# The sine written over the angle, the decays of the next pair fetched earlier, and VectorE making all rows of z in the first four steps

## The chip, the cores and the metric

The kernel runs on one core of one Trainium2 chip. The metric is the device time of one execution in microseconds (us). The core has five engines with their own instruction queues: TensorE (PE; its weight loads are listed as PEld), VectorE (DVE), ScalarE (ACT), GpSimd (POOL), and SyncE (SP), which here only issues DMA transfers. Each engine works through its queue in order, and semaphores hold an instruction until its operands are ready.

## The reference

Three stages in a row: a linear attention with complex decays over 768 tokens (4 batches, 8 heads, head size 48), a dense layer pair with a leaky unit, and a routed mixture of 8 experts, of which the first best one is taken per token.

```python
mag = sqrt(a_re * a_re + a_im * a_im)
scale = minimum(mag, 0.999) / (mag + 1e-06)
for t in range(768):
    S_re, S_im = ar * S_re - ai * S_im + k[t] (x) v[t], ar * S_im + ai * S_re
    y[t] = q[t] @ S_re
h = y @ w_in                     # 3072 x 384 @ 384 x 2048
x = (maximum(h, 0) + alpha * minimum(h, 0)) @ w_out
# mixture of experts on x: e = argmax(x @ w_gate + bias), out = p_e * (relu(x @ w1[e]) @ w2[e])
```

## The kernel before

**Steps and pairs.** The 768 tokens are cut into 6 chunks of 128, and with 4 batches there are 24 steps (k = 0 to 23). A step's attention is written with running products: with the scanned angle tau and the scanned magnitude (and its inverse) of the decays, the queries and keys are multiplied by cosine and sine of the angle and by these products. The result is z, a tile [128, 2, 3, 257]: for r = 0 (cosine) and r = 1 (sine), three sets of 128 key columns (L749) and 128 query columns (L751), and one column of the chunk's end. Steps are made in pairs (0,1), (2,3), ... (22,23); pairs (0,1) and (2,3) are handled in the opening.

**polar and polar_group.** polar() loads a pair's decays wa (real and imaginary part, 768 KB) and its queries and keys wq (768 KB). polar_group() then runs some 45 instructions on DVE, ACT and POOL over four work tiles m, x, s, e, whose names repeat from pair to pair with one buffer each: squares of wa on ACT (e, L664, and m, L665), an inverse root behind a table load (x, L670, and s, L671), products on DVE (L667, L673 to L679), the sign (L686) and arctangent (L691) in place in wa, the angle scans (L715, x <- wa) and their reduction by whole turns (L723, L725), the other scans, the cosine (L734, into e) and the sine (L735, into wa, whose real part is no longer needed). L742 keeps the last angle of a step for the next chunk (carry), and L749 and L751 write z. Tile wa has one buffer, so the next pair's wa can't be loaded until the last row of z that reads the sine is done. Pairs are written out as generators, from which one DVE instruction at a time is taken and set behind the dense layer's DVE instruction of that turn.

**After z.** SP sends z to DRAM (zd) and fetches it in another layout (qk). On PE each step's attention is pa (L782), the transposes pk (L790), copied by ACT to ks (L792), then py (L800, L802) and the state update pu (L814). Two steps fill xt, the input of one unit of the dense layer.

**The dense layer** goes through 12 units of 8 groups g. A group is ph (L843 to L846) on PE, n on ACT (L851), n on DVE (L853, two rows), gh on ACT (L856), gl on POOL (L858), and two groups later acc on PE (L878). In what follows gh_5 is the gh of the sixth group of a unit, and so on. Rows lt, mx, run, ix and the indirect load tbl (L237 to L260) are the routing of finished tokens; wraw, wf and w (L551 to L610) are the dense layer's weights, decoded during the opening; the last part of the kernel is the mixture of experts (L466 to L497). Which engine makes a row is set by side(mask), a test of a mask's bit that stands for the pair (bit 1, 2 for steps 0 and 1, 4 for pair (2,3), 8 for (4,5), 16 for the rest); with DZ = 15 a cosine row of L751 is on POOL for all pairs, and a sine row is on DVE for steps 0 to 5 and on POOL later.

Of the kernel before, what the change touches and what calls it, by code (L numbers as in the profile page):

```python
# [11 lines left out]
F32 = mybir.dt.float32  # L12
# [3 lines left out]
AF = mybir.ActivationFunctionType  # L16
ALU = mybir.AluOpType
PSUM = bass.MemoryType.PSUM

B, H, S, D = 4, 8, 768, 48  # L20
CH = 128
NC = S // CH
NSTEP = NC * B
# [52 lines left out]
DZ = 15  # L76
# [18 lines left out]
class Emit:  # L95
    def __init__(self, ctx, tc, aps):
        self.ctx, self.tc, self.nc = ctx, tc, tc.nc
        self.__dict__.update(aps)
        self.raws, self.vs, self.zs, self.zd, self.queue = {}, {}, {}, {}, None
        self.behind = None  # L100
        self.nwarm = 0
        self.paced = self.sine = None
        self.pacing = True
        self.scattered = []
        self.free = {"pa": ["pa0", "pa1"], "pq": ["pq0", "pq1"]}
# [512 lines left out]
    def polar(self, ks, split=False, apart=False):  # L618


        nc, ap_ = self.nc, self.ap_
        n, k0 = len(ks), ks[0]
        T = lambda nm, *sh, bufs=1: ap_.tile([128, *sh], F32, name=f"{nm}{k0}", tag=nm, bufs=bufs)
        W = 3 * CH
        if apart:

            wa, wq, *w = [self.wp.tile([128, 2, 2, W], F32, name=f"p{k0}_{i}", tag=f"w{NFC - 1 - i}") for i in range(4)]
            work = [w[i // 2][:, i % 2] for i in range(4)]
        else:
            wa, wq = T("wa", 2, 2, W), T("wq", 2, 2, W)  # L630
            work = None
        for lo, hi in [(i, i + 1) for i in range(n)] if split else [(0, n)]:
            self.dma(wa[:, lo:hi], self.pa_[k0 + lo:k0 + hi].rearrange("k p a t -> p k a t"))
            self.dma(wq[:, lo:hi], self.pq_[k0 + lo:k0 + hi].rearrange("k p a t -> p k a t"))
        return [ks, wa, wq, work]

    def polar_run(self, st, lo, hi, inline=False):
        ks, wa, wq, work = st
        if work is None:
            work = st[3] = [self.ap_.tile([128, 2, wa.shape[3]], F32, name=f"{nm}{ks[0]}", tag=nm, bufs=1) for nm in WORK]  # L640
        return self.polar_group(ks[lo:hi], wa[:, lo:hi], wq[:, lo:hi], [w[:, lo:hi] for w in work], inline)
# [14 lines left out]
    def polar_group(self, ks, wa, wq, work, inline):  # L656
        nc, ap_ = self.nc, self.ap_
        c = ks[0] // B
        ar, ai, q, kk = wa[:, :, 0], wa[:, :, 1], wq[:, :, 0], wq[:, :, 1]
        m2, x, s, e = work  # L660
        V, G, A = nc.vector, nc.gpsimd, nc.scalar
        bit = {0: 1, 1: 2, 2: 4, 4: 8}.get(ks[0], 16)
        side = lambda mask: G if mask & bit else V
# [45 lines left out]
        tau, pp, bb = x, m2, s  # L709
        t3 = lambda ap: ap.rearrange("p (j t) -> p j t", j=3)  # L710
# [11 lines left out]
        yield from scan(tau, "angle", ai, ALU.mult, ALU.add)  # L722
        A.activation(e, tau, AF.Identity, bias=self.magic)  # L723
        yield 1
        V.scalar_tensor_tensor(tau, e, MAGIC, tau, ALU.subtract, ALU.subtract)  # L725
        yield 1

        yield
# [1 line left out]
        yield from scan(pp, "decay", m2, ALU.max, ALU.mult)  # L730
        yield
        A.activation(e, tau, AF.Abs)
        sn, cs = ar, e
        A.activation(cs, e, AF.Sin, bias=self.hpi, scale=-2.0 * PI_LO)  # L734
        self.sine = A.activation(sn, tau, AF.Sin, scale=2.0 * PI_LO).ins  # L735
        side(GD).tensor_tensor(kk, kk, bb, ALU.mult)
# [1 line left out]
        side(~DQ).tensor_tensor(q, q, pp, ALU.mult)  # L738
        for i, k in enumerate(ks):
            yield  # L740
            if c < NC - 1:
                A.activation(self.carry[:, k % B], t3(tau[:, i])[:, :, CH - 1], AF.Identity, scale=-1.0)  # L742
            zp, zt = (self.wp, f"w{9 + k // 2}") if k in (1, 3) else (ap_, "z")
            z = zp.tile([128, 2, 3, 2 * CH + 1], F32, name=f"z{k}", tag=zt, bufs=ZB if zt == "z" else 1)
            end = t3(pp[:, i])[:, :, CH - 1]
            A.copy(self.pend[:, k, :], end)
            A.copy(z[:, :, :, CH], end.unsqueeze(1).to_broadcast([128, 2, 3]))
            for r, tr in enumerate((cs, sn)):
                self.last = V.tensor_tensor(z[:, r, :, CH + 1:], t3(kk[:, i]), t3(tr[:, i]), ALU.mult).ins  # L749
                yield 1  # L750
                side(~(DZ if r else 0)).tensor_tensor(z[:, r, :, :CH], t3(q[:, i]), t3(tr[:, i]), ALU.mult)  # L751
            self.zs[k] = z
            if inline:
                self.bounce(k)
                if not BB:
                    self.bounce_back(k)
# [329 lines left out]
def body(ctx, tc, aps):  # L1086
# [117 lines left out]
    def steps(text):  # L1204

        for part in re.findall("([^0-9 ]+)([0-9]*)", text):
            for c in part[0] * int(part[1] or 1):
                if c in "<>":
                    link[0] = c == "<"
                else:  # L1210
                    with em.behind_turn() if c in PT else nullcontext():
                        (chained if link[0] else step)(c)

    gens["p"], gens["C"] = polar(4, 5), attn_unit(2)
    steps(START)
    jobs, later = {}, {}
# [28 lines left out]
    for u in range(3, NU):  # L1245
        pg, ag = polar(2 * u, 2 * u + 1), attn_unit(u)
        p0 = max(NP * (u - 1) + PO, P0 + PS * (u - 2))
        width = PE_ if u < 6 else PW
        for i in range(PN):
            at(p0 + i * width // PN, pace if PACE & 1 else op, pg, d=later)  # L1250
        shift[u - 2] = max(0, p0 + width - NP * (u - 1))
        for i, m in enumerate(AT):
            at(NP * (u - 1) + shift[u - 2] + i, arun if PACE & 2 else run, ag, m)
# [127 lines left out]
```

## Time and profile before

| | before |
|---|---|
| runs | 992.59, 994.52, 1004.37 us; median 994.52 |
| profiled execution, device time | 996.86 us |
| its span in the trace | 995.1 us |
| mean granted clock of PE | 0.928 |
| busy: PE, PEld | 854.4 (86%), 807.5 (81%) |
| busy: DVE, ACT, POOL | 658.0 (66%), 478.3 (48%), 426.6 (43%) |
| DMA | 117.81 MB, mean 118 GB/s |
| loads of wa, of wq | 10 each, 768 KB, 10.2 and 8.6 us to landing |
| zd and qk | 24 each, 771 KB, 4.7 and 8.1 us to landing |

Busy time is the time in which an engine has an instruction running. A wait is put down to what ended it last ("PE pk <- ACT ks" is PE idle until ACT's copy ks). A row with several instructions (x4) shows its first start and the time to the last one's end. The granted clock is a share of full speed.

### The profile page before, as it was taken

The page shows a single profiled execution, that of the slowest core. Times are in us where ns is not written, and L with a number is a line of the kernel's source. Part 1 is how long each engine was busy: PE and PEld are TensorE (multiplying, and loading weights), DVE is VectorE, ACT ScalarE, POOL GpSimd, SP SyncE. Part 2 cuts the span into 40 slices and gives each one's busy share as a digit, 9 for nine tenths or more (in the row PEclk, how much of TensorE's full clock was granted, in tenths as well). Part 3 has the DMA queues.
Part 4 walks back from the last instruction along what each step waited for, and adds up shares of the span by engine and source line. Part 5 has one row for each costly group of instructions (what it writes and reads, how often), then busy time and mean ns, then how long its engine had stood idle before and what let it go on. Part 6 is the DMA issues. An engine that isn't in the chain of part 4 may idle for free. (4 is left out here: it accounts for less than half of the span.)

```text
span 995.1 us, 16140 instructions
## 1 busy us (share of the span) xinstructions
PE 854.4 (86%) x5948; PEld 807.5 (81%) x5948; DVE 658.0 (66%) x1264; ACT 478.3 (48%) x870; POOL 426.6 (43%) x339
## 2 busy tenths in 40 slices
PE   0655968897966999899899989898999999999994
PEld 0655958887965898889798989898999878889994
DVE  6986885779594959495968777784455464535561
ACT  7652556464454455363736464642234434434550
POOL 1135353436252634436463636462353264244451
PEclk9855977896997999999999999999999999999998
DMA  7816500242635251716243333423032445445560
GB/s 302 263 56 205 203 9 1 84 137 63 165 108 116 80 137 30 201 31 159 75 133 101 104 112 99 131 69 104 6 113 68 139 140 173 120 142 157 191 190 19
DMA packets 61290, 117.81 MB, mean 118 GB/s; under 512 B 10201, under 2 KB 39401, under 8 KB 61201
## 3 DMA queue, kind: packets, MB, share of 16 engines
q1 hardware_dynamic: 57232, 106.91, 36.3%
q0 software_dynamic: 3968, 9.77, 3.1%
q8 instruction: 49, 0.80, 0.4%
q14 instruction: 41, 0.33, 0.1%
HBM read 85.58 MB, written 28.91 MB: 115 GB/s over the span
## 5 line engine op out<-in xcount | busy, mean ns | idle before, releaser
L858 POOL TENSOR_TENSOR gl<-n,gh 128x512 fp32r<-128x512 f32 x96 | 143.6, 1498 | 224.1 <-ACT gh L856 111.3
L843 PE MATMUL ph<-xt,w 128*128 128x256 f32 x576 | 161.0, 306 | 17.1 <-DVE n L853 14.6
L878 PE MATMUL acc<-w,gh 128*128 128x392 f32 x768 | 165.4, 354 | 9.8 <-DVE lt L237 7.2
L844 PE MATMUL ph<-xt,w 128*128 128x256 f32 x576 | 155.1, 295 | 0.0
L878 PEld LDWEIGHTS acc<-w,gh 128*128 128x128 f32 x768 | 138.8, 197 | 11.6 <-DVE lt L237 8.4
L853 DVE SCALAR_TENSOR_TENSOR n<-n,al,ph 128x256 f32<-128x256 f32 x192 | 84.5, 474 | 87.7 <-ACT n L851 87.4
L843 PEld LDWEIGHTS ph<-xt,w 128*128 128x128 f32 x576 | 116.3, 202 | 19.9 <-DVE n L853 6.7
L844 PEld LDWEIGHTS ph<-xt,w 128*128 128x128 f32 x576 | 116.9, 203 | 0.2 <-issue 0.2
L846 PE MATMUL ph<-xt,w 128*128 128x256 f32 x576 | 106.9, 296 | 0.7 <-DVE w L559 0.7
L851 ACT ACTIVATE n<-ph 128x512 f32<-128x512 f32 x96 | 57.1, 595 | 100.3 <-PE ph L846 89.0
L856 ACT CAST gh<-n 128x512 fp32r<-128x512 f32 x96 | 59.4, 619 | 89.7 <-DVE n L853 82.9
L878 PE MATMUL acc<-w,gl 128*128 128x392 f32 x384 | 89.9, 350 | 11.9 <-POOL gl L858 11.9
L846 PEld LDWEIGHTS ph<-xt,w 128*128 128x128 f32 x576 | 88.4, 203 | 1.2 <-DVE w L559 1.0
L878 PEld LDWEIGHTS acc<-w,gl 128*128 128x128 f32 x384 | 71.4, 194 | 13.4 <-POOL gl L858 13.2
L782 PE MATMUL pa<-qk 96*128 96x128 f32 x384 | 58.2, 299 | 26.2 <-DMA qk<-zd 17.0
L782 PEld LDWEIGHTS pa<-qk 96*128 96x128 f32 x384 | 53.8, 210 | 30.3 <-DMA qk<-zd 12.3
L784 DVE TENSOR_TENSOR at<-pa,mask 128x512 f32<-128x512 f32 x48 | 32.7, 682 | 40.5 <-PE pa L782 34.4
L486 DVE SCALAR_TENSOR_TENSOR hls<-p2s,hhs 128x512 fp32r<-128x512 f32 x32 | 22.1, 689 | 38.3 <-ACT hhs L485 38.3
L260 POOL DMA_INDIRECT tbl<-tok,ix x24 | 25.5, 1064 | 50.4 <-DVE run L259 24.3
L800 PE MATMUL py<-at,v 128*64 128x128 f32 x384 | 44.5, 302 | 1.5 <-DVE at L784 1.1
L467 DVE TENSOR_TENSOR wls<-wrs,whs 128x768 fp32r<-128x768 f32 x20 | 28.2, 1409 | 25.6 <-ACT whs L466 25.6
L497 PE MATMUL a2s<-wls,hhs 128*128 128x384 f32 x128 | 43.7, 341 | 0.0
(334 smaller groups left out, 2034.2 us busy)
## 6 DMA issues: line engine op xcount, KB each, us to landing
zd<-z SPq DMA_DIRECT2D x24, 771.0 KB, 4.7
qk<-zd SPq DMA_DIRECT2D x24, 771.0 KB, 8.1
wraw<-in_w_io_dram SPq DMA_DIRECT2D x16, 768.0 KB, 12.3
wrs<-in_wcat_dram SPq DMA_DIRECT2D x32, 384.0 KB, 3.2
wrf<-in_wcat_dram SPq DMA_DIRECT2D x24, 384.0 KB, 3.6
wa<-in_pa__dram SPq DMA_DIRECT2D x10, 768.0 KB, 10.2
wq<-in_pq__dram SPq DMA_DIRECT2D x10, 768.0 KB, 8.6
v<-in_vv_dram SPq DMA_DIRECT2D x24, 200.0 KB, 2.4
```

Of the source, the lines that this page charges most:

```text
L497: nc.tensor.matmul(acc[t], x[:, 128 * t:128 * t + 128], w[:, DM:], start=(f == 0 and x is hh and w is wh), stop=(last and x is hl))
L782: nc.tensor.matmul(pa[:, i, :], kt[:, h, :], qt[:, h, :CH], start=True, stop=True)
L784: self.last = nc.vector.tensor_tensor(at, pa, self.mask.unsqueeze(1).to_broadcast([128, 4, CH]), ALU.mult).ins
L800: nc.tensor.matmul(o, v[:, h * D:h * D + 64], ats[g][:, i, :], start=True, stop=(c == 0))
L843: nc.tensor.matmul(ph[:, i, :], w1(fc, 0, c), xt[:, c, 0, :], start=(c == 0), stop=False)
L844: nc.tensor.matmul(ph[:, i, :], w1(fc, 0, c), xt[:, c, 1, :], start=False, stop=False)
L846: last = nc.tensor.matmul(ph[:, i, :], w1(fc, 1, c), xt[:, c, 0, :], start=False, stop=(c == 2)).ins
L851: nc.scalar.activation(nf, ph, AF.Relu, scale=-1.0)
L853: paced = nc.vector.scalar_tensor_tensor(nf[:, i, :], nf[:, i, :], self.al1[:, 2 * p + i:2 * p + i + 1], ph[:, i, :], ALU.mult, ALU.add).ins
L856: copy = nc.scalar.copy(gh, nf).ins
L858: rest = nc.gpsimd.tensor_tensor(gl, nf, gh.bitcast(F32), ALU.subtract).ins
L878: nc.tensor.matmul(acc[t][:, :XW], x[:, i, 128 * t:128 * t + 128], self.w[2 * p + i][:, h, DM:], start=(p == i == h == 0 and x is gh), sto ...
```

## The change

The sine is written over the angle (tile x) and no longer over wa, and the carry is kept at once when the angle is reduced, ahead of the other scans. For the pairs from (4,5) to (20,21) the load of the next pair's wa is written right behind the angle scans; polar() of that next pair then only loads wq. All rows of z of steps 0 to 3 go to DVE. Behind the third hunk's lines the code of polar_group goes on as before.

```diff
--- before.py
+++ after.py
@@ -96,6 +96,7 @@
     def __init__(self, ctx, tc, aps):
         self.ctx, self.tc, self.nc = ctx, tc, tc.nc
         self.__dict__.update(aps)
+        self.ahead, self.loaded = {}, None
         self.raws, self.vs, self.zs, self.zd, self.queue = {}, {}, {}, {}, None
         self.behind = None
         self.nwarm = 0
@@ -627,12 +628,22 @@
             wa, wq, *w = [self.wp.tile([128, 2, 2, W], F32, name=f"p{k0}_{i}", tag=f"w{NFC - 1 - i}") for i in range(4)]
             work = [w[i // 2][:, i % 2] for i in range(4)]
         else:
-            wa, wq = T("wa", 2, 2, W), T("wq", 2, 2, W)
+            wa = self.ahead.pop(k0, None) or T("wa", 2, 2, W)
+            wq = T("wq", 2, 2, W)
             work = None
+            if self.loaded == k0:
+                self.dma(wq, self.pq_[k0:k0 + n].rearrange("k p a t -> p k a t"))
+                return [ks, wa, wq, work]
         for lo, hi in [(i, i + 1) for i in range(n)] if split else [(0, n)]:
             self.dma(wa[:, lo:hi], self.pa_[k0 + lo:k0 + hi].rearrange("k p a t -> p k a t"))
             self.dma(wq[:, lo:hi], self.pq_[k0 + lo:k0 + hi].rearrange("k p a t -> p k a t"))
         return [ks, wa, wq, work]
+
+    def load_ahead(self, k):
+
+        wa = self.ahead[k] = self.ap_.tile([128, 2, 2, 3 * CH], F32, name=f"wa{k}", tag="wa", bufs=1)
+        self.dma(wa, self.pa_[k:k + 2].rearrange("k p a t -> p k a t"))
+        self.loaded = k
 
     def polar_run(self, st, lo, hi, inline=False):
         ks, wa, wq, work = st
@@ -722,7 +733,12 @@
         yield from scan(tau, "angle", ai, ALU.mult, ALU.add)
         A.activation(e, tau, AF.Identity, bias=self.magic)
         yield 1
+        if 4 <= ks[0] < NSTEP - 2:
+            self.load_ahead(ks[0] + 2)
         V.scalar_tensor_tensor(tau, e, MAGIC, tau, ALU.subtract, ALU.subtract)
+        if c < NC - 1:
+            for i, k in enumerate(ks):
+                A.activation(self.carry[:, k % B], t3(tau[:, i])[:, :, CH - 1], AF.Identity, scale=-1.0)
         yield 1
 
         yield
@@ -730,7 +746,7 @@
         yield from scan(pp, "decay", m2, ALU.max, ALU.mult)
         yield
         A.activation(e, tau, AF.Abs)
-        sn, cs = ar, e
+        sn, cs = tau, e
         A.activation(cs, e, AF.Sin, bias=self.hpi, scale=-2.0 * PI_LO)
         self.sine = A.activation(sn, tau, AF.Sin, scale=2.0 * PI_LO).ins
         side(GD).tensor_tensor(kk, kk, bb, ALU.mult)
@@ -738,8 +754,6 @@
         side(~DQ).tensor_tensor(q, q, pp, ALU.mult)
         for i, k in enumerate(ks):
             yield
-            if c < NC - 1:
-                A.activation(self.carry[:, k % B], t3(tau[:, i])[:, :, CH - 1], AF.Identity, scale=-1.0)
             zp, zt = (self.wp, f"w{9 + k // 2}") if k in (1, 3) else (ap_, "z")
             z = zp.tile([128, 2, 3, 2 * CH + 1], F32, name=f"z{k}", tag=zt, bufs=ZB if zt == "z" else 1)
             end = t3(pp[:, i])[:, :, CH - 1]
@@ -748,7 +762,7 @@
             for r, tr in enumerate((cs, sn)):
                 self.last = V.tensor_tensor(z[:, r, :, CH + 1:], t3(kk[:, i]), t3(tr[:, i]), ALU.mult).ins
                 yield 1
-                side(~(DZ if r else 0)).tensor_tensor(z[:, r, :, :CH], t3(q[:, i]), t3(tr[:, i]), ALU.mult)
+                side(~(15 if ks[0] < 4 else DZ if r else 0)).tensor_tensor(z[:, r, :, :CH], t3(q[:, i]), t3(tr[:, i]), ALU.mult)
             self.zs[k] = z
             if inline:
                 self.bounce(k)
```

In the order of SP's queue, with v the values, xt a copy that completes a unit's input, and the names' first number the step, the stretch around z of pair (12,13) stands thus before and after:

```order
L651 DMA qk12_3484<-zd12_3472 96x8x257
L651 DMA zd13_3482<-z13_3475 128x1542
L651 DMA wa14_3577<-in_pa__dram 128x2x768
L651 DMA qk13_3486<-zd13_3482 96x8x257
L651 DMA wq14_3578<-in_pq__dram 128x2x768
L651 DMA v14_3581<-in_vv_dram 128x400
L651 DMA v15_3583<-in_vv_dram 128x400
```

```order
L662 DMA qk12_3486<-zd12_3475 96x8x257
L662 DMA zd13_3484<-z13_3477 128x1542
L662 DMA wq14_3579<-in_pq__dram 128x2x768
L662 DMA qk13_3488<-zd13_3484 96x8x257
L662 DMA v14_3581<-in_vv_dram 128x400
L662 DMA wa16_3816<-in_pa__dram 128x2x768
L662 DMA v15_3583<-in_vv_dram 128x400
L823 DMA xt6_3602<-t3_12_3757 16x6x128 x2
```

The load of wa for a pair stood between zd and the second qk of the pair before it; now wq stands there, and wa of the pair after stands further on, between two loads of v and ahead of the copies to xt.

In the order of ACT's queue, at the end of the groups of unit 5 (n5_, gh5_) and the start of pair (16,17) (tiles e16, m216, x16, s16), with ks14 the copy of step 14's attention:

```order
L851 ACTIVATE n5_5_4021<-ph5_5_4002 128x512
L856 CAST gh5_5_4025<-n5_5_4021 128x512
L851 ACTIVATE n5_6_4088<-ph5_6_4069 128x512
L856 CAST gh5_6_4092<-n5_6_4088 128x512
L851 ACTIVATE n5_7_4127<-ph5_7_4108 128x512
L856 CAST gh5_7_4131<-n5_7_4127 128x512
L664 ACTIVATE e16_4158<-wa16_4147 128x768
L665 ACTIVATE m216_4155<-wa16_4147 128x768
L670 ACT_TABLE_LOAD
L670 ACTIVATE x16_4156<-e16_4158,tiny_75 128x768
L671 ACTIVATE s16_4157<-m216_4155,tiny_75 128x768
L792 COPY ks14_0_4185<-pk14_0_4180 128x384
```

```order
L865 ACTIVATE n5_5_4024<-ph5_5_4005 128x512
L870 CAST gh5_5_4028<-n5_5_4024 128x512
L675 ACTIVATE e16_4158<-wa16_3816 128x768
L681 ACT_TABLE_LOAD
L681 ACTIVATE x16_4156<-e16_4158,tiny_75 128x768
L865 ACTIVATE n5_6_4090<-ph5_6_4071 128x512
L870 CAST gh5_6_4094<-n5_6_4090 128x512
L865 ACTIVATE n5_7_4129<-ph5_7_4110 128x512
L870 CAST gh5_7_4133<-n5_7_4129 128x512
L682 ACTIVATE s16_4157<-m216_4155,tiny_75 128x768
L806 COPY ks14_0_4185<-pk14_0_4180 128x384
L697 ACTIVATE wa16_3816,oks_103<-wa16_3816,mth_89 128x2x384
```

The rows e, table load and x moved from behind gh5_7 to behind gh5_5, so ahead of n5_6; m moved further up (ahead of n5_4); s stays between gh5_7 and ks14_0.

In the order of DVE's queue, at z of step 2 (z2), among the rows that decode the weights wf2 and wf3; p2_3 holds the cosine, p2_0 before and p2_2 now the sine:

```order
L749 TENSOR_TENSOR z2_450<-p2_1_125,p2_3_127 128x3x128
L749 TENSOR_TENSOR z2_450<-p2_1_125,p2_0_124 128x3x128
L601 TENSOR_SCALAR wf2_456<-wf2_456 128x768
L601 TENSOR_SCALAR wf3_457<-wf3_457 128x768
L604 TENSOR_SCALAR wf2_456<-wf2_456 128x768
L604 TENSOR_SCALAR wf3_457<-wf3_457 128x768
L607 SCALAR_TENSOR_TENSOR wf2_456<-wraw2_138,wf2_456 128x768
L607 SCALAR_TENSOR_TENSOR wf3_457<-wraw3_140,wf3_457 128x768
L610 SCALAR_TENSOR_TENSOR wf2_456<-wraw2_138,wf2_456 128x768
L610 SCALAR_TENSOR_TENSOR wf3_457<-wraw3_140,wf3_457 128x768
L751 TENSOR_TENSOR z2_450<-p2_1_125,p2_0_124 128x3x128
L749 TENSOR_TENSOR z3_472<-p2_1_125,p2_3_127 128x3x128
```

```order
L763 TENSOR_TENSOR z2_451<-p2_1_125,p2_3_127 128x3x128
L765 TENSOR_TENSOR z2_451<-p2_1_125,p2_3_127 128x3x128
L763 TENSOR_TENSOR z2_451<-p2_1_125,p2_2_126 128x3x128
L602 TENSOR_SCALAR wf2_457<-wf2_457 128x768
L602 TENSOR_SCALAR wf3_458<-wf3_458 128x768
L605 TENSOR_SCALAR wf2_457<-wf2_457 128x768
L605 TENSOR_SCALAR wf3_458<-wf3_458 128x768
L608 SCALAR_TENSOR_TENSOR wf2_457<-wraw2_138,wf2_457 128x768
L608 SCALAR_TENSOR_TENSOR wf3_458<-wraw3_140,wf3_458 128x768
L611 SCALAR_TENSOR_TENSOR wf2_457<-wraw2_138,wf2_457 128x768
L611 SCALAR_TENSOR_TENSOR wf3_458<-wraw3_140,wf3_458 128x768
L765 TENSOR_TENSOR z2_451<-p2_1_125,p2_2_126 128x3x128
```

The second row here now is step 2's cosine row of L751, which POOL made before; the same holds for step 3, whose four rows follow. POOL's queue lost these two rows and those of steps 0 and 1.

## Rows read from the trace of the kernel before

**Rows 1.** Busy time by stretch: us, busy of PE, PEld, DVE, ACT, POOL; PEclk, DMA.
```profile
200.00:333.00 133.00, 105.90 (x767) 98.12 (x767) 98.36 (x183) 66.17 (x110) 56.54 (x38) 0.87 0.40 110
345.00:676.00 331.00, 301.49 (x2398) 289.76 (x2393) 243.81 (x475) 171.75 (x295) 164.01 (x119) 0.98 0.40 110
700.00:750.00 50.00, 50.00 (x373) 49.25 (x373) 24.70 (x90) 17.14 (x30) 22.54 (x19) 1.00 0.20 59
```

**Rows 2.** PE's waits, 200 to 333 us: us in total, times, longest.
```profile
PE acc L878 <- POOL gl L858: 8.9, 3, 5.7
```

**Rows 3.** PE's waits, 345 to 680 us.
```profile
PE acc L878 <- DVE lt L237: 7.2, 6, 2.1
PE pk L790 <- ACT ks L792: 6.8, 4, 2.0
PE pa L782 <- DVE mx L246: 6.2, 4, 1.5
PE pa L782 <- DMA qk<-zd: 5.5, 3, 2.8
```

**Rows 4.** Line L751 by form: duration ns min/median/max, first and last start.
```profile
L751 POOL TENSOR_TENSOR z<-p,p x2: 1309/8600/15892, 66.8 to 82.7; 128x384 f32<-128x384 f32 x2
L751 DVE TENSOR_TENSOR z<-p,p x2: 549/550/551, 72.8 to 74.2; 128x384 f32<-128x384 f32 x2
```

**Rows 5.** Timeline of DVE: start us, us, engine, line, operation [idle before].
```profile
72.78 0.55 DVE L751 TENSOR_TENSOR z<-p,p 128x384 f32<-128x384 f32 x1
...
74.19 0.55 DVE L751 TENSOR_TENSOR z<-p,p 128x384 f32<-128x384 f32 x1
...
94.81 0.69 DVE L784 TENSOR_TENSOR at<-pa,mask 128x512 f32<-128x512 f32 x1 [7.54 <-PE pa L782]
```

**Rows 6.** Timeline of POOL at the same place.
```profile
66.81 17.16 POOL L751 TENSOR_TENSOR z<-p,p 128x384 f32<-128x384 f32 x2 [36.75 <-DVE p L738]
```

**Rows 7.** Timeline of SP's DMA issues at the same place.
```profile
82.73 1.59 SPq L654 DMA_DIRECT2D zd<-z  x2
86.17 2.93 SPq L654 DMA_DIRECT2D qk<-zd  x2
```

**Rows 8.** Timeline of PE at the same place.
```profile
92.70 2.07 PE L782 MATMUL pa<-qk 96*128 96x128 f32 x8 [9.40 <-DMA qk<-zd]
```

**Rows 9.** Timeline of SP, pair (16,17) being loaded.
```profile
459.46 0.43 SPq L651 DMA_DIRECT2D wa<-in_pa__dram  x1
```

**Rows 10.** Timeline of ACT, the same period.
```profile
457.70 0.62 ACT L856 CAST gh<-n 128x512 fp32r<-128x512 f32 x1 [1.92 <-DVE n L853]
460.21 0.60 ACT L851 ACTIVATE n<-ph 128x512 f32<-128x512 f32 x1 [1.89 <-PE ph L846]
...
470.36 0.85 ACT L664 ACTIVATE e<-wa 128x768 f32<-128x768 f32 x1 [3.67 <-DMA wa<-in_pa__dram]
...
474.92 0.46 ACT L792 COPY ks<-pk 128x384 f32<-128x384 f32 x1
```

**Rows 11.** What engines idled for at tile wa: us, times, whole run.
```profile
  DMA wa<-in_pa__dram: 28.1, 10
```

**Rows 12.** Timeline of DVE, the same period: a scan and the last cosine row.
```profile
434.77 2.03 DVE L715 TENSOR_TENSOR_SCAN x<-first_angle,wa 128x384 f32<-128x384 bf16 x1
...
457.53 0.55 DVE L749 TENSOR_TENSOR z<-wq,e 128x384 f32<-128x384 f32 x1
```

**Rows 13.** Timeline of PE, the same period.
```profile
465.65 0.87 PE L878 MATMUL acc<-w,gl 128*128 128x392 f32 x4
...
468.06 0.49 PE L790 MATMUL pk<-ident,qk 96*128 96x96 f32 x4
...
475.43 0.55 PE L790 MATMUL pk<-ident,qk 96*128 96x96 f32 x4 [1.58 <-ACT ks L792]
```

**Rows 14.** Timeline of POOL near 302 us.
```profile
302.39 1.00 POOL L260 DMA_INDIRECT tbl<-tok,ix  x1 [5.10 <-DVE x L675]
```

**Rows 15.** Timeline of POOL, the period of rows 9.
```profile
462.50 1.29 POOL L858 TENSOR_TENSOR gl<-n,gh 128x512 fp32r<-128x512 f32 x1 [1.41 <-ACT gh L856]
```

## The prediction

> **What bounds the kernel now.** Durations come from the profiled execution, 996.86 us (span 995.1); the median of the three runs shown is 994.52, so it sits 2.34 us above the middle. I read the busy times by stretch first [rows 1]. From 700 to 750 us TensorE (PE) is busy all the time; nothing in the change reaches it there, and what is gained earlier can only move this block forward. From 200 to 333 us PE is busy 105.90 of 133 us at a mean granted clock of 0.87, from 345 to 676 it is busy 301.49 of 331. So 27.1 and 29.5 us of PE idleness lie in the stage in which the pairs of steps are prepared, and these, with idleness before 100 us, are all that the change can win. The list of PE's waits for the two stretches says who ends the idle time [rows 2, 3]: in the first above all the POOL rows gl (8.9 us in three waits), in the second ScalarE's (ACT's) ks (6.8 in four) and the qk load (5.5 in three, longest 2.8).
>
> **Part one: all rows of z on VectorE (DVE) for steps 0 to 3.** By line and form, two POOL rows z<-p,p of steps 2 and 3 took 1.309 and 15.892 us, while DVE's two took 0.55 each [rows 4]. The long one started at 66.81 [rows 6] and so ended at 82.70. DVE's last z row of step 3 ended at 74.74, and DVE worked on without a gap (its next wait, 7.54 us for PE, ends at 94.81, so it had been busy to 87.27) [rows 5]. The chain behind POOL's long row: zd issued 82.73, qk issued 86.17, PE's pa starts 92.70 after 9.40 us of idling [rows 7, 8]; from the end of the row to pa, 10.0 us. After the change the row is a DVE row, directly behind its neighbour, where each row costs a step of 0.47 us. (Step 2's last row is still behind the eight weight rows.) DVE's z row of step 2 began at 72.78 [rows 5], ends at 73.33, and one more row ahead makes that 73.8; plus 10.0 is 83.8, just behind the end of PE's earlier work at 83.3 (92.70 less 9.40). Gain 92.70 − 83.8 = 8.9. The two rows added to DVE cost 2 × 0.47 = 0.94 in a stretch in which DVE is fully busy and is waited for. Net −8.0. Lower bound of the gain 4: half of it, if the load qk, earlier, lands among more transfers. POOL only loses work by it.
>
> The page "SBUF — State Buffer" of the Trainium skill (section "SBUF: two separate sides") says that a VectorE operation with two inputs in SBUF and a GpSimd operation lock each other out of a shared pair of ports, and that the loser is fully blocked; the 15.892 us beside 1.309 for the same shape [rows 4] agree. The page "GPSIMD Engine Reference" (section "Elementwise — side-by-side cycle accounting") would price the move otherwise: GpSimd 1.96 times as slow as VectorE, no more. By that alone the move would save about 0.5 us a row and the sum would end some 7 us higher; the row decides.
>
> On steps 0 and 1 the same move swaps two POOL rows for two DVE rows at the very start, ahead of PE's first matmul. POOL's rows ran beside DVE's there, so no more can be won than about the 0.76 by which one such row is shorter on DVE [rows 4], and what DVE's own queue gains by it: −0.5, between 0 and −1.
>
> **Part two: the decays of the next pair.** Before, the load of wa stands behind z's rows, because the sine was in wa: issued 459.46; ACT's first row on it (e, L664) starts at 470.36, 3.67 us of this idle; over the run ACT idled 28.1 us for wa in 10 waits [rows 9 to 11]. After the change wa is free once the angle scans are done. The second scan of the pair before started at 434.77 and took 2.03, to 436.80 [rows 12], so the issue can move from 459.46 to about 437, and the load (10.9 us from its issue to e) has landed some 10 us before z ends. What holds e then is its own tile, which holds the cosine until the last cosine row of z on DVE (begun 457.53, 0.55 long, so to 458.08). So e can start at 458.3, behind gh_5, rather than at 470.36: 12 us of head start for each of nine pairs. No row of work is added: nine loads and the two carry rows of ACT of each pair stand earlier.
>
> Two prices follow. **ks.** ACT ran e, m, the table load, x and s as one block, 470.36 to 474.92, and the copy ks stood behind it; PE's pk, done once at 468.06, idled 1.58 us until 475.43 [rows 10, 13]. In the new order only s stands between gh_7 and ks, so the four waits (6.8) go. **qk.** A pair that starts earlier has its first qk earlier; the three waits of 5.5 us go, the last pair's 2.79 too. Together −12.3 at most, 0 at least, if other waits take over (PE's rows stand in the same order, and lt and mx rows of DVE are next: 7.2 and 6.2) [rows 3]. I take −10.
>
> **From 200 to 333 us** the pairs come closer together, DVE is busy for 98.36 of the 133 us [rows 1], and rows of different pairs collide. POOL's indirect load at 302.39 came after 5.10 us of waiting that ended with a DVE row of the pair's start (L675), and gl stands behind it [rows 14]; the longest of PE's waits for gl is 5.7 [rows 2]. In the new order gl_7 stands ahead of that load. Of the 27.1 idle, gl's 8.9 is the part that I see moved; the rest (rows of n and acc, scattered) can as well grow, since the pair's DVE rows are now issued sooner and stand ahead of some n rows. I take −8; +6 if DVE's collisions only change place, −25 if nearly all of the idleness goes and the clock of 0.87 with it.
>
> **The new wait.** In the new order e, the table load and x stand before n_6 on ACT, and gh_6, gl_6 and PE's acc wait behind that. Here gh_5 ended 458.32; e, load and x (the block's 4.56 from 470.36 to 474.92, less m and s, each about as long as e's 0.85: 2.9) end at 461.2; n_6 ran at 460.21 [rows 10], so it is 1.0 us late. gl_6 ended at 463.79 and PE's acc rows on gl came at 465.65 [rows 13, 15]: 1.86 us of slack cover it. Cost 0, as long as the last cosine row of z ends no more than 0.9 us behind gh_5; it ends 0.24 ahead.
>
> **Sum:** −0.5 − 8.0 − 10 − 8 = −26.5, and 996.86 − 26.5 = 970.4. Less the 2.34 by which the profiled run is long, 968; I forecast 970.
>
> **Rivals.** (1) *The head start is given back.* The pairs start 12 us earlier, but PE's order is fixed and each pair's later rows wait for the same lt, mx, at and n rows; only part one pays, with perhaps 2 us of ks. For it: DVE is busy 243.81 of 331 us too, and half of PE's idle time has other causes than wa. Against it: ks stands behind the load's block by order, and that order changes. 996.86 − 8.5 − 2 = 986, 984 on the median's basis. (2) *More than the sum.* The wait for wa was 28.1 us; if the whole stretch 200 to 333 loosens, 996.86 − 8.5 − 12.3 − 20 = 956. For it: most of PE's waits there end on an engine that works on a pair's rows. (3) *ACT blocks n_6*, the rival that ends slower. If that cosine row ends d behind gh_5, e waits on ACT's queue, and n_6, gh_6, gl_6 and acc are late by x = d + 1.0 − 1.86 in each of nine pairs, with ks and qk not won. With −8.5 from part one the time is above 996.86 from x = 0.94 (d = 1.8) and over 2% slower from x = 3.2 (d = 4.0); at x = 4 it is 996.86 − 8.5 + 36 = 1024. Against it: that row ends 0.24 us ahead of gh_5 in the period read. For it: gh_5 moves forward with PE as well, z need not. (4) *The change doesn't do what it says*: wa early, yet the pair starts no earlier, since e's tile is held by the cosine. That holds the start, but only to 458.3; so it ends as (1).
>
> **Chances.** Forecast 0.49 (own range 962 to 980, of which about a fifth lies above the 2% line at 974.6), (1) with (4) 0.30, (2) 0.15, (3) 0.06. About 2% of 994.52 is what a measurement here can tell from no change. Faster by over 2%: 0.38 + 0.15 = 0.53; within 2%: 0.11 + 0.30 = 0.41; slower 0.06. The range 954 to 989 takes in most of (1) and of (2) and leaves out (3) and the tails, some 0.15.
>
> **What would show it.** PE's 9.40 us before pa near 84 us gone, and qk issued near 77; if the gap stays, part one failed. ACT's wait for wa near 0 and e directly behind a gh; PE's waits for ks near 0 from 345 to 676; if these are gone and idleness there is still near 29 us, it is rival (1). A wait of ACT for z ahead of e, and PE waits for gl or gh at a group's seventh row, would be (3). Wrong altogether: PE not fully busy between 650 and 900 us, or more idle time in its last 50 us.

## The result and the profile after

The changed kernel took 950.68 us (median of 4 runs, 945.66 to 955.02) against 993.56 before (4 runs, 990.68 to 1004.37): the ratio is 0.9548, with a 95% interval of 0.9462 to 0.9634. So it is 4.5% faster, 43 to 45 us, where 26.5 had been forecast, and the time lies 3 us under the lower end of the range (954), which is less than the interval's half width of some 8.5 us. Its profiled execution took 951.42 us, 45.4 fewer than that of before.

| | before | after |
|---|---|---|
| profiled execution, device time | 996.86 us | 951.42 us |
| its span | 995.1 us | 949.6 us |
| mean granted clock of PE | 0.928 | 0.943 |
| busy: PE | 854.4 us (86%) | 838.5 us (88%) |
| busy: DVE, ACT, POOL | 658.0, 478.3, 426.6 us | 649.6, 479.2, 397.9 us |

To see where it went, the span is cut at the same places of the program, the first ph matmul of units 0, 1, 4 and 10 of the dense layer, and not at the same times:

| stretch | before | after | difference |
|---|---|---|---|
| start to unit 0 | 64.9 us | 63.6 us | −1.3 |
| unit 0 to unit 1 | 95.5 | 85.1 | −10.4 |
| units 1 to 3 (24 groups) | 201.1 | 183.3 | −17.8 |
| units 4 to 9 (48 groups) | 315.6 | 297.0 | −18.6 |
| unit 10 to the end | 318.0 | 320.6 | +2.6 |

The two middle stretches by busy time (columns as in [rows 1]), first of the kernel before:

```profile
160.40:361.50 201.10, 168.40 (x1206) 159.04 (x1205) 143.06 (x251) 103.14 (x178) 84.35 (x61) 0.89 0.39 110
361.50:677.10 315.60, 286.32 (x2276) 274.90 (x2276) 239.40 (x462) 164.98 (x285) 158.81 (x114) 0.98 0.37 102
```

and of the changed kernel:

```profile
148.70:332.00 183.30, 161.84 (x1206) 154.67 (x1205) 144.69 (x255) 104.59 (x182) 82.10 (x64) 0.92 0.45 121
332.00:629.00 297.00, 280.25 (x2279) 272.78 (x2277) 230.60 (x459) 164.30 (x282) 148.66 (x113) 0.98 0.39 109
```

PE does the same matmuls in both. In units 1 to 3 its idle time falls from 32.7 to 21.5 us (201.10 − 168.40, 183.30 − 161.84), and its busy time by 6.6 as well, at a granted clock of 0.92 instead of 0.89. In units 4 to 9 the idle time falls from 29.3 to 16.8 us, the busy time by 6.1. PE's waits there are now of one kind; this is the whole list of the changed kernel, 332 to 629 us, in place of [rows 3]:

```profile
PE pa L796 <- DMA qk<-zd: 15.8, 6, 3.4
PE pa L796 <- DVE at L798: 0.9, 1, 0.9
```

The waits for ks, lt and mx are gone, and those for qk have grown from 5.5 to 15.8 us. In the opening, where [rows 7, 8] had zd at 82.73, qk at 86.17 and 9.40 us of idling ahead of pa, the changed kernel's SP has

```profile
74.30 2.19 SPq L665 DMA_DIRECT2D zd<-z  x2
78.09 3.63 SPq L665 DMA_DIRECT2D qk<-zd  x2
```

and its PE

```profile
84.77 2.08 PE L796 MATMUL pa<-qk 96*128 96x128 f32 x8 [0.52 <-DMA qk<-zd]
```

At tile wa, where [rows 11] had 28.1 us in 10 waits for the load, the changed kernel shows (us idle, times; last line us from issue to landing, whose median was 10.0 before)

```profile
  POOL wq L754: 16.7, 8
...
  DVE z L763: 7.4, 4
...
  DMA wa<-in_pa__dram: 3.0, 2
...
DMA to landing us min/median/max: 3.1/4.5/5.5
```

So wa is in time. A new row stands above it: ACT's m (L676, a square of wa) waits 16.7 us in all for POOL's L754, which reads the tile that m is written to. One period of the changed kernel shows what hangs on that. ACT:

```profile
412.41 0.85 ACT L676 ACTIVATE m<-wa 128x768 f32<-128x768 f32 x1 [2.20 <-POOL wq L754]
413.16 0.58 ACT L865 ACTIVATE n<-ph 128x512 f32<-128x512 f32 x1
...
421.41 0.62 ACT L870 CAST gh<-n 128x512 fp32r<-128x512 f32 x1 [1.06 <-DVE n L867]
421.94 0.84 ACT L675 ACTIVATE e<-wa 128x768 f32<-128x768 f32 x1
```

DVE, whose rows of z stand behind its rows of n:

```profile
413.84 0.87 DVE L867 SCALAR_TENSOR_TENSOR n<-n,al,ph 128x256 f32<-128x256 f32 x2 [3.76 <-ACT n L865]
414.63 1.59 DVE L752 TENSOR_TENSOR wq<-wq,s 128x768 f32<-128x768 f32 x1
416.25 1.25 DVE L763 TENSOR_TENSOR z<-wq,e 128x384 f32<-128x384 f32 x1
```

SP and PE behind it:

```profile
419.22 0.32 SPq L662 DMA_DIRECT2D zd<-z  x1
...
422.75 0.33 SPq L662 DMA_DIRECT2D qk<-zd  x1
```

```profile
430.68 1.51 PE L796 MATMUL pa<-qk 96*128 96x128 f32 x8 [2.58 <-DMA qk<-zd]
```

As this period reads, m holds up ACT's n, n holds up DVE's n, that holds up z, and z holds up zd, qk and pa. The runs below test this. The rest of this period is as forecast: e (421.94) stands directly behind a gh and waits for nothing. So it is in the five pairs from (14,15) on; for the pairs (6,7) to (12,13) e waits 0.3 to 2.8 us for the last cosine row of z (the 7.4 us in four waits above).

### The profile page after: what moved, and what is told of

It reads as the page before. It is cut to its first block, busy times and chain, and to the rows that moved or that the text cites. A ratio compares the mean times of both kernels' runs of the same rounds, so it can differ in the third digit from the quotient of the medians.

```text
span 949.6 us, 16186 instructions
## 1 busy us (share of the span) xinstructions
PE 838.5 (88%) x5948; PEld 798.2 (84%) x5948; DVE 649.6 (68%) x1268; ACT 479.2 (50%) x870; POOL 397.9 (42%) x335
## 4 chain that ended last, share of the span: by engine, by line
PE 38%; DVE 20%; DMA 12%; issue 11%; POOL 5%; ACT 4%; SPq 0%; POOLq 0%; DVEq 0%; ACTq 0%
PE acc L892 7%; DMA qk<-zd 7%; PE a2s L498 6%; DMA zd<-z 4%; PE ph L857 3%; PE pa L796 3%; PE ph L858 3%; DVE n L867 3%; PE ph L860 3%; DVE z L763 2%; PE p2s L483 2%; PE p2s L479 2%; PE p2s L480 2%; POOL gl L872 1%; POOL wq L754 1%
## 5 line engine op out<-in xcount | busy, mean ns | idle before, releaser
L872 POOL TENSOR_TENSOR gl<-n,gh 128x512 fp32r<-128x512 f32 x96 | 150.9, 1573 | 208.1 <-ACT gh L870 100.3
L857 PE MATMUL ph<-xt,w 128*128 128x256 f32 x576 | 159.9, 304 | 14.2 <-DVE n L867 12.4
L892 PE MATMUL acc<-w,gh 128*128 128x392 f32 x768 | 160.5, 347 | 0.0
L858 PE MATMUL ph<-xt,w 128*128 128x256 f32 x576 | 153.3, 293 | 0.0
L892 PEld LDWEIGHTS acc<-w,gh 128*128 128x128 f32 x768 | 134.8, 191 | 0.8 <-issue 0.7
L857 PEld LDWEIGHTS ph<-xt,w 128*128 128x128 f32 x576 | 115.6, 201 | 16.6 <-DVE n L867 7.0
L860 PE MATMUL ph<-xt,w 128*128 128x256 f32 x576 | 105.3, 293 | 4.1 <-DVE w L560 4.1
L892 PE MATMUL acc<-w,gl 128*128 128x392 f32 x384 | 87.7, 344 | 3.1 <-POOL gl L872 3.0
L584 POOL TENSOR_TENSOR w<-of,w 128x8 fp32r<-128x8 f32 x16 | 10.1, 652 | 92.6 <-ACT w L583 92.6
```

What stands on the lines that cost most here:

```text
L857: nc.tensor.matmul(ph[:, i, :], w1(fc, 0, c), xt[:, c, 0, :], start=(c == 0), stop=False)
L858: nc.tensor.matmul(ph[:, i, :], w1(fc, 0, c), xt[:, c, 1, :], start=False, stop=False)
L860: last = nc.tensor.matmul(ph[:, i, :], w1(fc, 1, c), xt[:, c, 0, :], start=False, stop=(c == 2)).ins
L872: rest = nc.gpsimd.tensor_tensor(gl, nf, gh.bitcast(F32), ALU.subtract).ins
L892: nc.tensor.matmul(acc[t][:, :XW], x[:, i, 128 * t:128 * t + 128], self.w[2 * p + i][:, h, DM:], start=(p == i == h == 0 and x is gh), sto ...
```

## The experiments

The theory to be tested, A, has three parts: the two parts of the change add up; in units 1 to 3 a pair's chain (load, start, z, zd, qk) is what PE waits for in the end, so that every microsecond of an earlier start counts; and in units 4 to 9 what the late start cost was also in the waits for lt, mx and at. Its rival is the forecast's account: some single collisions of rows, of which an early start clears a few.

The table gives the median, the ratio to the runs of before in the same job with its 95% interval, and the five stretches of the profiled execution. The first stretch varies between executions of one program (last section). The others vary too: over the four profiled executions of the changed program (after, e5, e9 and e12) by 4.6, 3.6, 1.3 and 3.2 us, and in units 4 to 9, where e2, e4 and e11 have the rows of the changed kernel in the same order, all seven lie between 292.2 and 299.4. So differences of 5 us, and there of 7, are not read, the +2.6 behind unit 10 among them.

| run | median us | ratio (interval) | to unit 0 | to unit 1 | units 1–3 | units 4–9 | rest |
|---|---|---|---|---|---|---|---|
| before | 993.56 | | 64.9 | 95.5 | 201.1 | 315.6 | 318.0 |
| after | 950.68 | 0.9548 (0.9462–0.9634) | 63.6 | 85.1 | 183.3 | 297.0 | 320.6 |
| e1_only_z | 985.16 | 0.9876 (0.9835–0.9918) | 56.9 | 89.0 | 202.3 | 317.7 | 319.1 |
| e2_only_wa | 954.21 | 0.9606 (0.9533–0.9679) | 58.3 | 90.9 | 183.5 | 292.2 | 318.9 |
| e3_early_only | 963.81 | 0.9686 (0.9627–0.9745) | 55.9 | 85.4 | 183.1 | 316.9 | 321.7 |
| e4_late_only | 969.40 | 0.9737 (0.9670–0.9804) | 62.2 | 89.5 | 205.0 | 292.7 | 321.5 |
| e5_after_again | 952.46 | 0.9521 (0.9439–0.9603) | 56.4 | 86.7 | 186.9 | 296.8 | 323.8 |
| e6_wa_behind_zd | 983.28 | 0.9864 (0.9778–0.9949) | 58.3 | 87.6 | 194.7 | 315.3 | 320.9 |
| e7_m_behind_e | 941.33 | 0.9403 (0.9322–0.9483) | 63.3 | 87.6 | 182.5 | 289.8 | 325.3 |
| e8_po10 | 960.91 | 0.9601 (0.9519–0.9682) | 63.7 | 84.8 | 190.0 | 298.4 | 322.3 |
| e9_after_5 | 952.75 | 0.9526 (0.9478–0.9573) | 56.2 | 89.7 | 186.5 | 297.9 | 321.2 |
| e10_m_behind_e_5 | 945.77 | 0.9429 (0.9379–0.9479) | 64.3 | 84.4 | 185.2 | 287.3 | 322.4 |
| e11_early_behind_zd | 966.76 | 0.9655 (0.9604–0.9706) | 63.7 | 87.1 | 195.7 | 299.4 | 321.0 |
| e12_wa_behind_sine | 958.44 | 0.9567 (0.9510–0.9624) | 55.7 | 85.3 | 186.6 | 298.1 | 321.7 |

The kernel of e7 ran again as e10; the profiled execution of e7 is its longest, 950.35 us.

**Without a run: which lines do it.** With the call of load_ahead taken out, and only the sine written over the angle and the carry moved, the built program has the same rows in the same order on all five engines as the changed kernel. The library that lays out the program puts the load at the place where its tile has become free; the lines that write it there change nothing. What did the work is that the sine left wa. (The layout moves other rows too when a tile comes free at another time, so every edit below tests a load together with the order of the queues that goes with it.)

**One part alone.** e1 is the kernel before with one line changed:

```diff
-                side(~(DZ if r else 0)).tensor_tensor(z[:, r, :, :CH], t3(q[:, i]), t3(tr[:, i]), ALU.mult)
+                side(~(15 if ks[0] < 4 else DZ if r else 0)).tensor_tensor(z[:, r, :, :CH], t3(q[:, i]), t3(tr[:, i]), ALU.mult)
```

> The kernel before with part one alone: all rows of z of steps 0 to 3 on DVE; sine and loads as before. The whole change took the profiled time from 996.9 to 951.4 us, of which 11.7 us had been won by the first group of unit 1 (160.4 to 148.7). Theory A (the two parts add up, and what is won by 160 us is kept to the end): 984 to 988 us, PE's 9.4 us wait for qk near 90 us gone. Rival (the head start of the opening is given back where the pairs of steps are what PE waits for, between 200 and 345 us): 992 or more.

e2 is the changed kernel with this line put back.

> The changed kernel with part two alone: the sine over the angle and the early load; the cosine rows of z of steps 0 to 3 stay on POOL. Theory A (adding up): 960 to 964 us, the waits before 100 us as in the kernel before. Rival (the two parts need each other, since the early start of pair (4,5) is what lets the next pairs close up): 970 or more.

e1 came to 985.16, as the theory said, and its PE shows no wait ahead of the pa that had waited 9.40 us:

```profile
81.53 1.97 PE L782 MATMUL pa<-qk 96*128 96x128 f32 x8
```

Its middle stretches (202.3 and 317.7) are those of before: what the opening wins is neither given back nor multiplied there. e2 came to 954.21, 6 us under its range, and has the middle stretches of the changed kernel (183.5, and 292.2 where that has 297); the opening's wait and POOL's long row are back (line L765 by form, then PE):

```profile
L765 POOL TENSOR_TENSOR z<-p,p x2: 1310/8604/15897, 60.2 to 76.1; 128x384 f32<-128x384 f32 x2
```

```profile
86.14 2.08 PE L796 MATMUL pa<-qk 96*128 96x128 f32 x8 [9.42 <-DMA qk<-zd]
```

The ratios give 12.4 us for part one and 39.3 for part two, 51.6 together, against 45 to 48 for the whole in three jobs (0.9548, 0.9521, 0.9526). The two intervals, about 4 and 7 us to either side, hold that difference, so they add up as far as this tells.

**Early and late pairs.** In e3 the sine leaves wa only up to pair (8,9), in e4 only from pair (10,11) on:

```diff
-        sn, cs = tau, e
+        sn, cs = tau if ks[0] < 10 else ar, e        # e3
+        sn, cs = ar if ks[0] < 10 else tau, e        # e4
```

(The call of load_ahead is bound to the same pairs.)

> The changed kernel, but the sine goes over the angle only up to pair (8,9), so that the pairs (6,7), (8,9) and (10,11) get their decays early and the pairs from (12,13) on get them as before. Theory A (between 150 and 345 us the chain of a pair is the bound, since a pair is set to every five groups there and takes longer than these; each pair's wait for wa counts in full): about 30 us are won by the first group of unit 4 (361.5 to 332) and the later pairs need 52.5 us each as before: 966 to 970 us. Rival (the forecast's: some 8 us in that stretch, the rest from the later pairs): 976 to 980 us.

> The changed kernel, but the sine goes over the angle only from pair (10,11) on, so that the pairs from (12,13) on get their decays early, the three pairs ahead of them as before. Theory A: the first group of unit 4 comes some 12 us early, pairs then take 49.5 to 50 us instead of 52.5: 966 to 970 us, and together with the run of the early pairs alone this adds up to the whole. Rival (the forecast's split): 974 to 978 us for 10 us in the later pairs and 8 before.

e3 came to 963.81, 2 us under its range, and e4 to 969.40, inside it. By the medians alone the rival of e4 (974 to 978) is not excluded, since its interval reaches from 964 to 977 us; the stretches decide. They are separate. e3 has units 1 to 3 in 183.1 us and units 4 to 9 in 316.9, e4 205.0 and 292.7. The first group of unit 4 came 4.8 us early in e4 (361.5 to 356.7), not 12 as its expectation had it. With part one in both, the gains add up: 31.3 + 26.2 − 12.4 = 45.1 us. And e3's waits of PE from 324 to 641 us bring back what the changed kernel had lost:

```profile
PE pa L796 <- DMA qk<-zd: 5.9, 3, 2.9
PE acc L892 <- DVE lt L238: 5.6, 4, 1.6
PE pa L796 <- DVE mx L247: 5.5, 4, 1.5
PE pk L804 <- ACT ks L806: 5.0, 4, 2.5
```

So lt and mx, which the forecast had taken for the next waits in line, belong to the pair's late start, with the order of rows that goes with it, as ks does. That these short rows of DVE then stand in a queue with the pair's long ones would explain it; no run shows this by itself.

**A load that lands some microseconds too late.** e6 holds the load of wa behind the first zd of the pair ahead, e11 does this only for the pairs (6,7), (8,9) and (10,11):

```diff
             if inline:
                 self.bounce(k)
+                if 4 <= k < NSTEP - 2 and k == ks[0]:        # e11: 4 <= k < 10, later pairs as in the change
+                    with self.tc.issue_after(self.sent):     # sent: the zd transfer that bounce(k) has just issued
+                        self.load_ahead(k + 2)
```

> The changed kernel, but the load of the next pair's wa is held behind the first zd of the pair, so some 22 us later than in the changed kernel: it lands about 8 us after the last cosine row of z, where the kernel before had e start 12 us after that row and the changed kernel at once. Theory A (the microseconds of the pair's start count, one for one, where pairs are the bound, and nearly so later): about a third of part two's 42 us stays, 975 to 983 us, and ACT's first row of a pair waits for wa 5 to 9 us. Rival (a threshold: any start ahead of the next unit's first group clears the collisions of ks, lt and mx): 960 us or less.

> The changed kernel, but for the pairs (6,7), (8,9) and (10,11) the load of wa is held behind the first zd of the pair ahead; the later pairs as in the changed kernel. Theory A (in the stretch of units 1 to 3 a pair's start counts one for one): the 24 groups from unit 1 to unit 3 take about 195 us, 11 more than in the changed kernel and 6 fewer than before, the later units 297 as in the changed kernel: 960 to 965 us. Rival (that stretch is bound by single collisions, which any early start clears): 950 to 956 us.

e6 came to 983.28, just above what was expected, e11 to 966.76, 2 us above it. In units 1 to 3 they took 194.7 and 195.7 us, between the 201 to 205 of the kernels whose loads are late there (before, e1, e4) and the 183 to 187 of those whose loads are early (after, e2, e3, e5, e9, e12). The 195 us expected for e11 were set with e6 known, so e11 repeats that stretch and is no second forecast of it. For the pairs (6,7), (8,9) and (10,11) e started 6.7 to 7.3 us behind the last cosine row of z in e11 and 0.1 in the changed kernel, before 14.0, 16.5 and 4.8: some 40% of the head start is left on the mean (none of it for the third), and about the same share of the gain. That fits a gain by the microsecond; a threshold that one or two of the three pairs pass would fit as well. In units 4 to 9 the theory did not hold for e6: 315.3 us is all the time of before, though e starts sooner than before. One period of e6 shows why. ACT:

```profile
434.68 0.60 ACT L867 ACTIVATE n<-ph 128x512 f32<-128x512 f32 x1 [1.65 <-PE ph L862]
439.58 0.85 ACT L675 ACTIVATE e<-wa 128x768 f32<-128x768 f32 x1 [4.30 <-DMA wa<-in_pa__dram]
440.33 0.60 ACT L872 CAST gh<-n 128x512 fp32r<-128x512 f32 x1
```

and its DVE and PE:

```profile
444.45 0.87 DVE L869 SCALAR_TENSOR_TENSOR n<-n,al,ph 128x256 f32<-128x256 f32 x2 [8.26 <-ACT n L867]
```

```profile
448.33 2.08 PE L798 MATMUL pa<-qk 96*128 96x128 f32 x8 [6.72 <-DMA qk<-zd]
```

e stands here between n and gh of a unit's seventh group (in the changed kernel ahead of that n) and waits for the load, with gh and the next n behind it; over the run ACT waits 29.8 us for wa in 10 waits, the longest 5.9 (5 to 9 us for each had been expected), and PE's waits for qk in units 4 to 9 are 26.4 us (those for lt and mx don't come back with the load's lateness alone). The forecast's third rival has the same blocking of ACT by e, there with the cosine row for its cause: a place of e ahead of a gh is a gain only while wa is there before e's turn. e6 also has everything of the change but the early load, and its ratio, 0.9864, is that of part one alone (0.9876): what part two wins hangs on when the load lands. In the changed kernel the load is issued 25 us ahead of e (396.73 and 421.94 in the period shown) and takes 4.5.

**The new wait of m.** e7, and e10 with more rounds, put m behind e on ACT:

```diff
-        A.activation(e, ar, AF.Square)
-        A.activation(m2, ai, AF.Square)
+        sq = A.activation(e, ar, AF.Square).ins
+        with self.tc.issue_after(sq) if ks[0] > 4 else nullcontext():
+            A.activation(m2, ai, AF.Square)
```

> The changed kernel with one order on ACT turned round: the square m stands behind e, and no longer ahead of n of a unit's fifth group, where it waited 2.2 us for POOL's row L754 (16.7 us in 8 waits) and held up n, DVE's z rows behind n, and so zd and qk. Theory A (this is what makes PE wait 2.5 to 3.4 us for qk at each pair, 20.8 us in all): these waits fall below 8 us, and the time to 938 to 944. Rival (qk is late for the pair's own length, and m only fills a gap): the waits stay, 947 to 955 us.

> The changed kernel, beside the next run for a direct comparison. 947 to 955 us.

> The changed kernel with the square m behind e on ACT, again, with more rounds: its last profile had PE's waits for qk halved (21.3 to 10.5 us) and 290 instead of 297 us for the 48 groups from unit 4 to unit 9. Theory A (m ahead of n held up z and qk): 7 to 11 us under the changed kernel in the same job. Rival (chance): within 3 us of it.

e7 came to 941.33 us, inside its range, beside 952.46 for the changed kernel in its job (e5). With more rounds e10 took 945.77 us and the changed kernel (e9) 952.75; the ratios are 0.9429 and 0.9526, and their intervals just touch. All ten runs of e7 and e10 average 943.5 us, the sixteen of the changed program (with e5, e9 and e12) 952.9. The 48 groups of units 4 to 9 took 287.3 us in e10 and 289.8 in e7, against 297.9 in e9, and e10's waits of PE there were

```profile
PE pa L797 <- DMA qk<-zd: 7.7, 5, 2.9
PE pa L797 <- DVE at L799: 1.8, 3, 0.9
```

In the seven executions with m's old place PE's waits for qk there are 11.1 to 16.6 us and the stretch never under 292.2. So about half of the waits for qk came by way of m, and this version is faster than the changed kernel by about 1%, and than the one before by 5.7%. The other half is left; below 8 us, as expected, only in this stretch.

**Setting the pairs one group earlier.** e8 changes one number of the order, `PO = -9` to `PO = -10`.

> The changed kernel with the pairs from (12,13) on set one group earlier in the order. Theory A (with wa early, a pair can start earlier still, and the wait for qk is a matter of where the order sets the pair): PE's waits for qk from 345 us on near 0, 935 to 944 us. Rival (the next pair's tiles come free too late, so the rows only wait in DVE's and ACT's queues and hold up n and gh): 950 us or more, with PE waiting for n or gh.

e8 came to 960.91, no better than the changed kernel: its median lies 8 us above that of e5, but 7 of this is the first stretch in the profiled executions, and the intervals overlap. The waits for qk went, as the theory said, but others took their place; PE from 338 to 637 us:

```profile
PE py L814 <- DVE at L798: 10.2, 7, 1.8
PE pk L804 <- ACT ks L806: 3.4, 5, 0.7
```

The rival was nearer: in DVE's queue more of a pair's rows now stand ahead of at (wq and the first two rows of z, for the second at of a step). n and gh, which it named, are not in the list.

**Two repeats.** e5 is the changed kernel again.

> The changed kernel once more, beside the next three. 947 to 955 us. In its profile of before, the stretch 46 to 62 us ran at half clock and the first group of unit 0 came at 63.6 us; in three of the four experiments so far that stretch ran near full clock and the group came at 56 to 58 us. If that is chance and not the kernel, this run shows either.

> The changed kernel, but the load of the next pair's wa is held behind the sine rather than the angle scans, some 8 us later in a pair. Theory A (what counts is that wa has landed when the last cosine row of z is done; between the angle scans and that row there are 26 us, and the load takes 4.5 to 10 us): no change, 947 to 956 us. Rival (every microsecond of an earlier load counts): 8 us for each of nine pairs in part, 965 us or more.

e5 took 952.46 us. e12 is no test of its theory: its edit binds only rows of ACT, the sine's engine, and the load is issued by SP. The built program has the same rows in the same order on all five engines as the changed kernel, and SP issued the load 14.1 us after the first group of unit 5, in the changed kernel 13.9. So it is the changed kernel once more, 958.44 us (949.17 to 961.69) where e9 in the same job took 952.75, and says what medians of four runs are good for here: 6 us apart without a cause in any stretch. How late wa may be without harm was not measured.

## Why the prediction was wrong

**The direction and the mechanisms held, the sizes did not.** Part one, the freeing of wa, e directly behind gh_5, the end of the waits for ks and for wa, and no loss by e ahead of n_6 all came as forecast. The sum of 26.5 us was too small by 16 to 19. Its first paragraph counted only PE's idle time as what can be won; in the two middle stretches 23.8 us of idle time went, and 12.6 us of PE's own busy time with it (6.6 and 6.1), a term that the sum put at nothing.

**Part one (−8.5).** Alone it gave 12.4 us by the ratio (8.2 to 16.5 by its interval) and 6.5 in the stretch from unit 0 to unit 1, where its place is (95.5 to 89.0; the changed program took 85.1 to 89.7 there, so what part two adds can't be read). The chain of zd, qk and pa moved by 8 us as worked out (92.70 to 84.77). As far as this tells, the term was sized right.

**Units 1 to 3 (the term for 200 to 333 us, −8): the step that failed first.** It took the idle time as single collisions and credited the one whose rows I could see move (gl, 8.9). That one went, and the stretch won twice as much: about 18 us, from the early pairs alone (e3). PE's longest waits there before were, beside gl,

```profile
PE ph L843 <- DVE n L853: 11.5, 4, 4.1
PE pk L790 <- ACT ks L792: 3.3, 1, 3.3
PE pos L253 <- DVE run L259: 2.7, 1, 2.7
```

and in the changed kernel

```profile
PE ph L857 <- DVE n L867: 8.9, 3, 3.8
PE pa L796 <- DMA qk<-zd: 4.5, 2, 3.7
PE py L814 <- DVE at L798: 3.3, 1, 3.3
PE pk L804 <- DVE at L798: 2.9, 1, 2.9
```

The waits for gl and ks are gone, that for run nearly so, most of those for n have stayed, and others for qk and at have come. What fits this, together with e6 and e11, is that a pair is set to every five groups there and that its chain sets the pace, through whatever row happens to be last; this is argued from the stretches, and that one cause stands behind all the names is not shown. Of the 17.8 us, 11.2 are idle time and 6.6 are PE's own rows. The other early kernels agree: PE is busy there for 162 to 165 us, in the late ones for 168 to 169. The granted clock (0.92 instead of 0.89) explains only a part, since e5 has the shorter busy time (164.4) at 0.89 as well. The forecast had named the clock only for the case in which nearly all goes.

**Units 4 to 9 (−10, of at most 12.3): the second.** The cap was wrong. It counted the waits for ks and qk and called lt and mx the ones that would take over. They went too (7.2 and 6.2 us, 13.4 together, with 2.9 for at), since e3 brings them back with the late start. And the waits for qk did not go but became the bound, 15.8 instead of 5.5 us. Two errors of opposite sign; that their balance, 12.5 us of idle time, lies so near the cap of 12.3 is luck. The rest is 6.1 us of busy time. Why PE's busy time fell by 6 there, at the same mean clock of 0.98 to two places, the runs do not settle.

**The wait not foreseen.** ACT's order showed m "further up", and the prediction passed over it. It cost some 7 to 9 us (e10 against e9, and the means of all runs), by way of n, z and qk. The prediction had checked e, the table load and x against z's rows on DVE; m had to be checked in the same way against POOL's L754.

**The rivals.** The second, more than the sum, was the one that happened, with the wrong account of its size (956). The first, the gain given back, is excluded by e3 and e4. The third's blocking is real, and e6 shows it, from a late load. In the changed kernel its condition, a late cosine row, is met a little in four pairs (7.4 us of ACT's time), with no wait of PE for gl or gh behind it in units 1 to 9; from (14,15) on it is not met, as the forecast said. The fourth names the row that now sets the start (e follows 0.1 us behind the last cosine row in each of the nine pairs), but the pairs start earlier all the same.

## What to carry to other kernels

When a chain that repeats is set among another stream's work in fixed order, add up all waits of the stretch before you decide which belong to the chain: the last row named in a wait can be only where the lateness came out, as lt and mx were here. A tile's last reader decides where the next load can go; writing a result over another tile, one that is dead at the end anyway, moved the load by more than 20 us without a row of work more, and no line that asks for the early load was needed. A row moved up in a queue is free only if its operands and its target are there by then; check each such row, not only the one that the change is about.

## What the runs showed of the hardware that was not expected

The granted clock of PE in the opening differs between executions of one program, and some 7 us go with it. In the profiled execution of the changed kernel it was at half (1.2 GHz) from 46 to 54 us:

```profile
46.00:54.00 8.00, 8.00 (x46) 7.44 (x46) 4.10 (x7) 1.70 (x5) 0.00 (x0) 0.50 0.70 272
```

and in e5, the same kernel again, near full (2.4 GHz):

```profile
46.00:54.00 8.00, 5.05 (x55) 4.68 (x55) 7.59 (x13) 4.28 (x8) 0.00 (x0) 0.97 0.71 270
```

55 matmuls in 5.05 us here, 46 in 8.00 there. Ahead of it, from 30 to 38 us, PE was busy 7.41 us here and 8.00 there, at full clock both times; the clock was down by 46 us there (0.52 from 42 to 46 us) and by 54 us here (0.93 from 50 to 54, 0.50 behind it). The first group of unit 0 then came at 63.6 and at 56.4 us. Over all profiles that place fell at 55.7 to 58.3 us (seven of them) or at 62.2 to 64.9 (seven, the one of e8 and that of before among them); the granted clock from 46 to 54 us is 0.84 to 1.00 in the first seven and 0.50 in each of the others. Both groups hold kernels with and without either part of the change, so it is no effect of the change. Comparisons of whole profiled executions carry this; the stretches behind it don't. What makes the clock fall sooner in one execution than in another is open.

POOL's row of 128 by 384 took 15.9 us twice, in the kernel before and in e2, while DVE worked without a gap; the other rows of this line on POOL took at most 1.7 us in the kernel before. It lasted through some two dozen rows of DVE, and it ended, both times, 0.1 us behind the end of two rows n, although DVE went on:

```profile
81.74 0.87 DVE L853 SCALAR_TENSOR_TENSOR n<-n,al,ph 128x256 f32<-128x256 f32 x2
82.52 1.87 DVE L601 TENSOR_SCALAR wf<-wf 128x768 f32<-128x768 f32 x2
```

n reads ph, which PE writes; the DVE rows that POOL's row lasted through read no such tile. The two rows behind n took 1.87 us, where the same pair took 1.02 at 74.65: there POOL's next row of z ran (1.31 us). So a POOL row beside a busy DVE costs neither its own length nor always that of DVE's whole run; which rows of DVE hold it up, the runs show only at this one place of the program.
